# Building weight signs with an OR on VectorE, squaring on VectorE, and a list schedule with other durations, in an attention + two feed-forward layers kernel

## The chip, the cores and the metric

One core of a Trainium2 chip. The metric is the device time of one execution in microseconds (us); the figure to predict is the median of several runs. The engines are called by the profile's names: PE (TensorE), ACT (ScalarE), DVE (VectorE), POOL (GpSimd), SP (the queue that issues the transfers).

## The reference

Attention with 2 x 12 heads, 448 tokens and head size 64, with tanh-capped scores, then two feed-forward layers over 896 tokens. All inputs are fp32.

```python
scores = cap * np.tanh((scale * q @ k.T) / cap)
attn = softmax(scores) @ v            # -> x: 896 tokens x 768
h = x @ w_in                          # 768 x 2048, first layer
x = (np.maximum(h, 0) + alpha * np.minimum(h, 0)) @ w_out
h = x @ w_in2                         # second layer
r = np.maximum(h, 0)
out = (r * r) @ w_out2                # 896 x 768
```

## The kernel before, in words

Attention runs first (to about 102 us of the span), with the first three weight columns of the first layer prepared beside it (`fetch`, `advance`, `up_now`; they use `read`, lines 173 to 185). None of this is touched.

The two layers follow. Work is transposed: features lie on the 128 partitions, tokens (2 halves b of S = 448) in the free dimension. A product of fp32 accuracy is made of three passes of reduced-precision matmuls: weight and token operands are split into a rounded high part (wh, xh, a copy on ACT, line 254) and a rest (wl, xl, a subtraction on DVE, line 257), and `multiply` (line 198) issues high x high, high x low, low x high. The up product of one column group f is 6 x 3 matmuls of 448 tokens for each b, into one PSUM bank (`up`). In the first layer ACT evacuates the bank twice (relu, line 270, and relu of the negative, line 272) and DVE joins them with the slope (line 273). In the second, ACT takes the relu (line 270) and squares it in place (line 276). The down products (`down`) use Strassen-Winograd's seven products of quarter matrices: A11, S3 = A11 - A21, A12 and A22 are loaded as 4 quarters of 4 parts (`quarter`), sums of weights and tokens are DVE additions (line 249), and one product (P1) is done in plain fp32 (line 195) without a split.

The host passes each weight as a 64-bit pattern of which the kernel makes fp32 numbers. A load (`load`, line 219) has five steps: a 768 KB transfer into one of two raw buffers (line 223); ACT multiplies the high words by 2^-112 into w, the rebias (line 239); DVE shifts the low words right by 29 (line 240); ACT writes the sign into the low word, as a 16-bit float with stride four made of the high word times 2^-60 (line 233, called by the operation in line 241); DVE joins, w << 3 | low (line 237). The raw buffer is then free. 61 loads are made this way, 13 + 16 for the up layers and 2 x 16 quarters. There are 16 w buffers, 3 pairs wh/wl outside attention's, 8 PSUM banks and one buffer t.

The order of all this is not written by hand. `layers` describes every operation to `Plan` (`op`), with an engine and a cost in us; `Plan.order` runs a list schedule: an engine that is idle takes, of its operations that are ready and whose buffers are to be had, the one that comes first in the program. A result is ready for others a lag after its end. The instructions are issued in that order, and on the chip each engine keeps it strictly. The costs are `act(n)`, `dve(n)` (two rates) and fixed figures for matmuls (0.2044 us each, 0.752 for a plain fp32 product); the sign is charged like the rebias, act(768) + 0.06 = 0.875 us.

Of the kernel before, what the change touches and what calls it, by code (L numbers as in the profile page):

```python
# [13 lines left out]
ALU = mybir.AluOpType  # L14
# [3 lines left out]
P = 128  # L18
# [10 lines left out]
PARTS = 4  # L29
# [2 lines left out]

PLAIN = ("P1",)

SLOTS = {"raw": 2, "w": 16, "wh": 3, "wl": 3, "g": 35, "t": 1, "xh": 4, "xl": 4}


# [15 lines left out]
class Plan:  # L53
# [4 lines left out]
    def tag(self, name, tiles):  # L58
        self.free[name], self.queue[name] = list(tiles), []

    def op(self, engine, cost, emit, reads=(), writes=(), port=False, lag=0.06):
        op = Op(len(self.ops), engine, cost, emit, port, lag)
        self.ops.append(op)
        before = []
        for buf in reads:
            before.append(buf.writer)
        for buf in writes:
            before += [buf.writer, *buf.readers]
        for other in set(before):
            if other is not None and other is not op:  # L70
                other.feeds.append(op)
                op.needs += 1
        for buf in reads:
            buf.readers.append(op)
        for buf in writes:
            buf.writer, buf.readers = op, []
            if not buf.taken:
                buf.taken = True
                op.takes.append(buf)
                self.queue[buf.tag].append(op)  # L80
        op.bufs = list(dict.fromkeys([*reads, *writes]))
        for buf in op.bufs:
            buf.left += 1

    def order(self):
# [5 lines left out]
        for op in self.ops:  # L91
            if not op.needs:
                heapq.heappush(events, (0.0, op.number, "ready", op))
        while events:
            now = events[0][0]
            while events and events[0][0] <= now:
                _, _, what, op = heapq.heappop(events)
                if what == "ready":
                    heapq.heappush(ready[op.engine], (op.number, op))
                elif what == "end":  # L100
                    for buf in op.bufs:
                        buf.left -= 1
                        if not buf.left and buf.tag:
                            self.free[buf.tag].append(buf.tile)
                    for other in op.feeds:
                        other.needs -= 1
                        if not other.needs:
                            heapq.heappush(events, (now + op.lag, other.number, "ready", other))
# [36 lines left out]
class Net:  # L145
# [65 lines left out]
        self.activate(self.early_g[f], self.early_t, ps, f)  # L211

    def act(self, n):
        return 0.17 + 0.00084 * n

    def dve(self, n, rate=1):
        return 0.16 + 0.00103 * n if rate == 1 else 0.13 + 0.00052 * n

    def load(self, src):

        nc, plan, n = self.nc, self.plan, self.NC * P
        raw, w = Buf("raw"), Buf("w")
        plan.op("SP", 0.06, lambda: nc.sync.dma_start(raw.tile, src), (), [raw], lag=4.0)
        low, high = Buf(), Buf()
        for b in (low, high):
            b.writer = raw.writer

        def parts():
            return self.words(raw.tile)

        def sign():
            halves = raw.tile.bitcast(F16).rearrange("p n (f t) -> p n f t", t=4)
            nc.scalar.mul(halves[:, :, :, 1], parts()[1].bitcast(F32), 2.0 ** -60)  # L233

        def join():
            bits = w.tile.bitcast(I32)
            nc.vector.scalar_tensor_tensor(bits, bits, 3, parts()[0], op0=ALU.logical_shift_left, op1=ALU.bitwise_or)  # L237

        plan.op("ACT", self.act(n) + 0.06, lambda: nc.scalar.mul(w.tile, parts()[1].bitcast(F32), 2.0 ** -112), [high, raw], [w])  # L239
        plan.op("DVE", self.dve(n, 2), lambda: nc.vector.tensor_scalar(parts()[0], parts()[0], 29, None, op0=ALU.logical_shift_right), [raw], [low], port=True)  # L240
        plan.op("ACT", self.act(n) + 0.06, sign, [high, raw], [low])
        plan.op("DVE", self.dve(n), join, [low, w, raw], [w], port=True)
        return w

# [13 lines left out]
        return h, l  # L258

    def products(self, ps, w, x, c, first, last):  # L260
        self.plan.op("PE", 3 * 0.2044 if len(w) == 2 else 0.752, lambda: self.multiply(ps.tile, [b.tile for b in w], [b.tile for b in x], c, first, last),
                     [*w, *x], [ps])

    def up(self, w, f, b, first):

        nc, S, plan, half = self.nc, self.S, self.plan, self.NF // 2
        ps, g, t = Buf("ps"), Buf("g"), Buf("t")
        for c in range(self.NC):
            self.products(ps, w, self.x[b, c], c, c == 0, c == self.NC - 1)
        plan.op("ACT", self.act(S), lambda: nc.scalar.activation(g.tile, ps.tile, AF.Relu), [ps], [g])  # L270
        if first:
            plan.op("ACT", self.act(S), lambda: nc.scalar.activation(t.tile, ps.tile, AF.Relu, scale=-1.0), [ps], [t])  # L272
            plan.op("DVE", self.dve(S), lambda: nc.vector.scalar_tensor_tensor(
                g.tile, t.tile, self.slope_t[:, f:f + 1], g.tile, op0=ALU.mult, op1=ALU.add), [t, g], [g], port=True)
        else:
            plan.op("ACT", self.act(S), lambda: nc.scalar.square(g.tile, g.tile), [g], [g])  # L276
        self.g[b, f] = g
        if b == 1 and f >= half:
            self.sum(self.g[1, f - half], g, self.g[1, f - half], "tensor_sub", S)

    def quarter(self, name, i):
        a = {"A11": 0, "S3": 1, "A12": 2, "A22": 3}[name]
        w = self.a[name, i] = self.load(self.wdown[:, a * PARTS + i])
        if name == "S3":
            self.sum(w, self.a["A11", i], w, "tensor_sub", self.NC * P)

# [73 lines left out]
    def layers(self):  # L360

        both = range(self.B)
        self.x = {(b, j): [Buf(None, t[b][:, j]) for t in (self.xh, self.xl)] for b in both for j in range(self.NC)}
        self.g = {(0, f): Buf(None, self.early_g[f]) for f in range(AHEAD)}
        ahead = []
        for f in range(AHEAD):
            hl = []
            for tag, t in (("wh", self.wh[f]), ("wl", self.wl[f])):
                b = Buf(tag, t)
                b.taken = True  # L370
                hl.append(b)
            ahead.append(hl)
        for first, src, self.wdown in ((True, self.w1, self.w2), (False, self.w3, self.w4)):
            self.a = {}
            for f in range(self.NF):
                early = first and f < AHEAD
                w = ahead[f] if early else self.split(self.load(src[:, f]), ("wh", "wl"), self.NC * P)
                for b in both:
                    if not (early and b == 0):
                        self.up(w, f, b, first)  # L380
            for i in range(PARTS):
                self.quarter("A11", i)
                self.quarter("S3", i)
            for name in ("A12", "A22"):
                for i in range(PARTS):
                    self.quarter(name, i)
            self.down(not first)
        engines = {mybir.EngineType.PE, mybir.EngineType.Activation, mybir.EngineType.DVE, mybir.EngineType.Pool, mybir.EngineType.SP}
        with self.tc.manual_schedule(engines=engines):
            for op in self.plan.order():  # L390
                op.emit()
# [331 lines left out]
    def run(self, fast):  # L723
        self.raws = []
        with ExitStack() as ctx:
            wp = self.pool(ctx, "wp", 1)
            splits = {t: [wp.tile([P, self.NC, P], F32R, name=f"{t}{n}") for n in range(SLOTS[t])] for t in ("wh", "wl")}
            self.wh, self.wl = splits["wh"], splits["wl"]
# [23 lines left out]
            plan.tag("raw", [self.raw[:, (AHEAD + n) % 2] for n in range(2)])  # L752
            plan.tag("w", [lp.tile([P, self.NC, P], F32, name=f"w{n}") for n in range(SLOTS["w"])])
            for t in ("wh", "wl"):
                plan.tag(t, splits[t][AHEAD:])
            plan.tag("t", [self.early_t])
            plan.tag("g", [lp.tile([P, self.S], F32, name=f"g{n}") for n in range(SLOTS["g"])])
            for t in ("xh", "xl"):
                plan.tag(t, [lp.tile([P, self.S], F32R, name=f"{t}{n}") for n in range(SLOTS[t])])
            banks = [hm.tile([P, self.S], F32, name=f"hm{n}", padded_shape=[P, 512]) for n in range(2)]  # L760
# [67 lines left out]
```

## Time and profile before

| | us |
|---|---|
| median of 3 runs | 566.67 |
| lowest to highest | 564.88 to 567.07 |
| the profiled execution | 567.58 |
| its span | 565.8 |
| PE busy | 538.9 (95%) |
| ACT busy | 419.6 (74%) |
| DVE busy | 405.4 (72%) |
| transfers, mean | 114 GB/s |

All durations of the working are from the profiled execution. The 1.8 us between its time and its span lie around the program. A busy PE here means that matmuls are in its pipeline; two records of 370 ns follow each other every 204 ns. The stages are read from the kernel's loops: up products of the first layer from 102 to 219 us, its down products to 323, up products of the second to 449, its down products to 560.

### The profile page before, as it was taken

What the parts mean: (1) busy time and instruction counts of PE and PEld (TensorE: products, weight loads), DVE (VectorE), ACT (ScalarE), POOL (GpSimd) and SP (SyncE); (2) the same over time, 40 slices, a digit from 0 to 9 for tenths busy, and PEclk for the clock granted to TensorE, in tenths of its full rate; (3) what the DMA queues carried; (4) which work ended last, traced back from release to release, by engine and by line L of the source; (5) the groups of instructions that cost most, each with busy time, mean ns of one, the idle gap of its engine ahead of it and who ended that gap; (6) DMA issues with size and microseconds to landing.
All of it is one profiled execution on the core that took longest, in us unless ns stands there. A gap on an engine that the chain in (4) does not pass through costs nothing.

```text
span 565.8 us, 6752 instructions
## 1 busy us (share of the span) xinstructions
PE 538.9 (95%) x2556; PEld 424.9 (75%) x2556; DVE 405.4 (72%) x574; ACT 419.6 (74%) x518; POOL 2.0 (0%) x12
## 2 busy tenths in 40 slices
PE   7889899979999997998999899999999999999996
PEld 2223345969999896758898788999999984789985
DVE  1798999465567767889999964444567579989862
ACT  6999892487889878957655479999889997354550
POOL 1000000000000000000000000000000000000000
PEclk9999999999999999999999899999999999999998
DMA  6455442053454444553000035555444553010111
GB/s 198 175 175 168 133 130 59 0 168 117 162 167 120 160 144 138 166 162 116 1 2 0 0 112 168 167 168 167 137 149 162 167 168 111 2 49 2 49 50 54
DMA packets 19576, 64.23 MB, mean 114 GB/s; under 512 B 3920, under 2 KB 10576, under 8 KB 19536
## 3 DMA queue, kind: packets, MB, share of 16 engines
q1 hardware_dynamic: 19392, 63.72, 34.8%
q8 instruction: 22, 0.36, 0.3%
q14 instruction: 18, 0.15, 0.1%
q10 hardware_dynamic: 144, 0.00, 0.0%
HBM read 60.89 MB, written 2.79 MB: 113 GB/s over the span
## 4 chain that ended last, share of the span: by engine, by line
PE 48%; ACT 28%; DVE 16%; DMA 4%; issue 2%; POOL 0%; ACTq 0%; DVEq 0%; POOLq 0%
PE ps L198 28%; ACT raw L233 14%; PE hm L198 11%; DVE w L237 3%; PE ps L195 3%; ACT wh L254 3%; PE pv L516 3%; ACT w L239 3%; DMA k<-in_kT 2%; DVE wl L257 2%; ACT g L270 2%; PE ps L466 2%; DVE raw L240 2%; DVE w L249 2%; ACT xh L254 1%
## 5 line engine op out<-in xcount | busy, mean ns | idle before, releaser
L198 PE MATMUL ps<-x,wh 128*128 128x448 f32 x576 | 166.6, 370 | 3.9 <-ACT t L272 2.7
L233 ACT ACTIVATE raw<-raw 128x768 f16<-128x768 f32 x61 | 118.5, 1943 | 22.8 <-DVE raw L240 22.8
L237 DVE SCALAR_TENSOR_TENSOR w<-w,raw 128x768 int32<-128x768 int32 x61 | 58.5, 959 | 88.1 <-ACT raw L233 88.0
L198 PEld LDWEIGHTS ps<-x,wh 128*128 128x128 f32 x576 | 108.3, 189 | 17.7 <-ACT t L272 3.6
L198 PE MATMUL ps<-x,wl 128*128 128x448 f32 x288 | 106.4, 369 | 0.4 <-DVE wl L257 0.4
L254 ACT CAST xh<-g 128x448 fp32r<-128x448 f32 x93 | 52.9, 576 | 62.9 <-PE ps L198 40.9
L198 PE MATMUL ps<-xh,wh 128*128 128x448 f32 x224 | 83.9, 374 | 6.7 <-ACT t L272 3.0
L257 DVE TENSOR_TENSOR wl<-w,wh 128x768 fp32r<-128x768 f32 x77 | 73.5, 955 | 16.4 <-ACT wh L254 15.0
L198 PE MATMUL ps<-xl,wh 128*128 128x448 f32 x224 | 82.2, 367 | 0.8 <-DVE xl L257 0.8
L198 PE MATMUL ps<-xh,wl 128*128 128x448 f32 x224 | 82.3, 367 | 0.4 <-DVE wl L257 0.4
L254 ACT CAST wh<-w 128x768 fp32r<-128x768 f32 x77 | 64.8, 842 | 6.4 <-DVE w L237 4.9
L257 DVE TENSOR_TENSOR xl<-g,xh 128x448 fp32r<-128x448 f32 x93 | 56.4, 621 | 11.5 <-ACT xh L254 10.3
L198 PEld LDWEIGHTS ps<-x,wl 128*128 128x128 f32 x288 | 54.5, 189 | 5.3 <-DVE wl L257 0.7
L239 ACT ACTIVATE w<-raw 128x768 f32<-128x768 f32 x61 | 56.1, 919 | 2.0 <-DMA raw<-in_w 2.0
L198 PE MATMUL hm<-x,wh 128*128 128x448 f32 x192 | 54.6, 366 | 0.0
L198 PEld LDWEIGHTS ps<-xh,wh 128*128 128x128 f32 x224 | 42.2, 188 | 14.9 <-ACT t L272 3.6
L198 PEld LDWEIGHTS ps<-xl,wh 128*128 128x128 f32 x224 | 42.2, 189 | 4.7 <-DVE xl L257 1.2
L198 PEld LDWEIGHTS ps<-xh,wl 128*128 128x128 f32 x224 | 42.2, 188 | 4.3 <-DVE wl L257 0.7
L481 ACT ACTIVATE E<-ps,scale_t 128x896 f32<-128x896 f32 x42 | 40.3, 1022 | 5.3 <-PE ps L466 5.3
L249 DVE TENSOR_TENSOR g<-g,g 128x448 f32<-128x448 f32 x64 | 39.0, 620 | 1.0 <-ACT g L276 0.7
L198 PEld LDWEIGHTS hm<-x,wh 128*128 128x128 f32 x192 | 36.0, 187 | 3.4
L486 ACT ACTIVATE E<-E,cap_t 128x1792 f32<-128x1792 f32 (+1 forms) x24 | 38.1, 1617 | 0.0
(96 smaller groups left out, 630.7 us busy)
## 6 DMA issues: line engine op xcount, KB each, us to landing
raw<-in_w SPq DMA_DIRECT2D x64, 768.0 KB, 4.2
out_T<-g SPq DMA_DIRECT2D x12, 224.0 KB, 2.0
k<-in_kT SPq DMA_DIRECT2D x11, 224.0 KB, 4.9
q<-in_qT SPq DMA_DIRECT2D x11, 224.0 KB, 5.1
v<-in_vT SPq DMA_DIRECT2D x6, 384.0 KB, 5.2
rb<-row SPq DMA_DIRECT2D x10, 224.0 KB, 3.7
vt<-in_vt SPq DMA_DIRECT2D x6, 64.0 KB, 5.6
r<-rows SPq DMA_DIRECT2D x20, 1.8 KB, 3.6
```

The lines of the kernel that those rows point to most:

```text
L195: self.nc.tensor.matmul(ps, w[0][:, c, :], x[0], start=first, stop=last)
L198: self.nc.tensor.matmul(ps, a[:, c, :], m, start=first and n == 0, stop=last and n == 2)
L233: nc.scalar.mul(halves[:, :, :, 1], parts()[1].bitcast(F32), 2.0 ** -60)
L237: nc.vector.scalar_tensor_tensor(bits, bits, 3, parts()[0], op0=ALU.logical_shift_left, op1=ALU.bitwise_or)
L239: plan.op("ACT", self.act(n) + 0.06, lambda: nc.scalar.mul(w.tile, parts()[1].bitcast(F32), 2.0 ** -112), [high, raw], [w])
L240: plan.op("DVE", self.dve(n, 2), lambda: nc.vector.tensor_scalar(parts()[0], parts()[0], 29, None, op0=ALU.logical_shift_right), [raw], [l ...
L249: plan.op(engine, cost, lambda: getattr(e, op)(out.tile, a.tile, b.tile), [a, b], [out], port=True)
L254: plan.op("ACT", self.act(n), lambda: nc.scalar.copy(h.tile, w.tile), [w], [h])
L257: lambda: e.tensor_sub(l.tile, w.tile, h.tile.bitcast(F32)), [w, h], [l], port=True)
L481: nc.scalar.activation(es[-1][:, n % 2], ps, AF.Tanh, scale=self.scale_t)
L486: self.nc.scalar.activation(x, x, AF.Exp, scale=self.cap_t)
L516: nc.tensor.matmul(self.pv[u][rows, g, :], self.v[u][0][:, g, c, rows], self.chunk(u, g * FULL + c)[:, e], start=c == 0, stop=False)
```

## The change

- `load` takes a flag, half. Where it is true the load is as before. Where it is false, DVE makes the sign: the high words are ANDed in place with the sign bit (which must come after the rebias has read them), then low = low >> 29 | high in one operation, then the join as before. ACT then has only the rebias.
- `HALF` says which: false for all up loads; for the quarters true for A11 and A12 (a = 0, 2) and false for S3's load and A22 (a = 1, 3).
- `SQ` is false for every f: the square is g = max(ps, 0) * g on DVE, read from PSUM, instead of a square on ACT.
- The planner's figures change: act, dve, the sign's cost (1.68), the matmuls' (0.2038 and 0.746) and the default lag (0.15 for 0.06). Its rules stay.

```diff
+HALF = (lambda f, first: False, lambda i, a: i % 2 == 0)
+SQ = lambda f: False
...
-    def op(self, engine, cost, emit, reads=(), writes=(), port=False, lag=0.06):
+    def op(self, engine, cost, emit, reads=(), writes=(), port=False, lag=0.15):
...
     def act(self, n):
-        return 0.17 + 0.00084 * n
+        return 0.05 + 0.000885 * n
     def dve(self, n, rate=1):
-        return 0.16 + 0.00103 * n if rate == 1 else 0.13 + 0.00052 * n
-    def load(self, src):
+        return 0.075 + 0.00103 * n if rate == 1 else 0.07 + 0.00052 * n
+    def load(self, src, half):
...
-        plan.op("DVE", self.dve(n, 2), lambda: nc.vector.tensor_scalar(parts()[0], parts()[0], 29, None, op0=ALU.logical_shift_right), [raw], [low], port=True)
-        plan.op("ACT", self.act(n) + 0.06, sign, [high, raw], [low])
+        if half:
+            plan.op("DVE", self.dve(n, 2), lambda: nc.vector.tensor_scalar(parts()[0], parts()[0], 29, None, op0=ALU.logical_shift_right), [raw], [low], port=True)
+            plan.op("ACT", 1.68, sign, [high, raw], [low])
+        else:
+            plan.op("DVE", self.dve(n, 2), lambda: nc.vector.tensor_scalar(parts()[1], parts()[1], -(1 << 31), None, op0=ALU.bitwise_and), [raw], [high], port=True)
+            plan.op("DVE", self.dve(n), lambda: nc.vector.scalar_tensor_tensor(
+                parts()[0], parts()[0], 29, parts()[1], op0=ALU.logical_shift_right, op1=ALU.bitwise_or), [raw, high], [low], port=True)
         plan.op("DVE", self.dve(n), join, [low, w, raw], [w], port=True)
...
-        self.plan.op("PE", 3 * 0.2044 if len(w) == 2 else 0.752, ...
+        self.plan.op("PE", 3 * 0.2038 if len(w) == 2 else 0.746, ...
...
-            plan.op("ACT", self.act(S), lambda: nc.scalar.square(g.tile, g.tile), [g], [g])
+            if SQ(f):
+                plan.op("ACT", self.act(S), lambda: nc.scalar.square(g.tile, g.tile), [g], [g])
+            else:
+                plan.op("DVE", self.dve(S) + 0.06, lambda: nc.vector.scalar_tensor_tensor(
+                    g.tile, ps.tile, 0.0, g.tile, op0=ALU.max, op1=ALU.mult), [g, ps], [g])
...
-        w = self.a[name, i] = self.load(self.wdown[:, a * PARTS + i])
+        w = self.a[name, i] = self.load(self.wdown[:, a * PARTS + i], HALF[1](i, a))
...
-                w = ahead[f] if early else self.split(self.load(src[:, f]), ("wh", "wl"), self.NC * P)
+                w = ahead[f] if early else self.split(self.load(src[:, f], HALF[0](f, first)), ("wh", "wl"), self.NC * P)
```

## Rows read from the trace of the kernel before

**Rows 1.** Busy time by stage: length, busy us of PE, PEld, DVE, ACT, POOL, clock, DMA.

```profile
102.00:219.00 117.00, 110.18 (x527) 99.29 (x525) 73.64 (x104) 95.32 (x121) 0.00 (x0) 0.99 0.42 135
219.00:323.00 104.00, 100.32 (x434) 82.02 (x435) 93.23 (x143) 69.47 (x100) 0.00 (x0) 0.99 0.21 69
323.00:449.00 126.00, 125.66 (x612) 114.63 (x612) 69.53 (x96) 111.91 (x137) 0.00 (x0) 1.00 0.47 151
449.00:560.00 111.00, 108.83 (x489) 91.16 (x487) 88.00 (x134) 62.88 (x90) 0.00 (x0) 1.00 0.18 62
```

**Rows 2.** The same table for the two stretches with a low granted clock.

```profile
126.00:130.00 4.00, 4.00 (x15) 3.58 (x14) 2.23 (x4) 2.97 (x4) 0.00 (x0) 0.63 0.16 68
320.00:324.00 4.00, 4.00 (x13) 3.57 (x13) 3.48 (x6) 1.30 (x2) 0.00 (x0) 0.57 0.00 0
```

**Rows 3.** TensorE's timeline, gaps: start, us, instruction, in brackets idle time and releaser.

```profile
114.24 0.68 PE L198 MATMUL ps<-x,wh 128*128 128x448 f32 x2 [0.92 <-ACT wh L254]
...
125.00 0.67 PE L198 MATMUL ps<-x,wh 128*128 128x448 f32 x2 [1.87 <-ACT t L272]
...
186.42 0.68 PE L198 MATMUL ps<-x,wh 128*128 128x448 f32 x2 [0.79 <-ACT t L272]
...
219.10 0.47 PE L198 MATMUL ps<-xh,wh 128*128 128x448 f32 x1 [2.98 <-ACT t L272]
...
256.04 0.47 PE L198 MATMUL ps<-xh,wh 128*128 128x448 f32 x1 [1.44 <-ACT g L332]
...
318.76 0.47 PE L198 MATMUL ps<-xh,wh 128*128 128x448 f32 x1 [1.44 <-ACT wh L254]
```

**Rows 4.** Groups by line and shape: count, busy us, mean ns, idle time before.

```profile
L233 ACT ACTIVATE raw<-raw 128x768 f16<-128x768 f32 x61 | 118.5, 1943 | 22.8 <-DVE raw L240 22.8
...
L239 ACT ACTIVATE w<-raw 128x768 f32<-128x768 f32 x61 | 56.1, 919 | 2.0 <-DMA raw<-in_w 2.0
...
L237 DVE SCALAR_TENSOR_TENSOR w<-w,raw 128x768 int32<-128x768 int32 x61 | 58.5, 959 | 88.1 <-ACT raw L233 88.0
...
L240 DVE TENSOR_SCALAR raw<-raw 128x768 int32<-128x768 int32 x61 | 33.9, 556 | 0.1
...
L276 ACT ACTIVATE g<-g 128x448 f32<-128x448 f32 x32 | 18.6, 581 | 0.4
...
L181 DVE TENSOR_SCALAR raw<-raw 128x768 int32<-128x768 int32 x3 | 1.6, 530 | 0.0
...
L183 DVE SCALAR_TENSOR_TENSOR raw<-raw 128x768 int32<-128x768 int32 x3 | 3.0, 992 | 0.1
```

**Rows 5.** ScalarE's timeline near 110 and near 217.

```profile
109.07 0.54 ACT L270 ACTIVATE g<-hm 128x448 f32<-128x448 f32 x1 [4.89 <-PE hm L198]
...
110.36 1.95 ACT L233 ACTIVATE raw<-raw 128x768 f16<-128x768 f32 x1
112.03 0.65 ACT L272 ACTIVATE t<-hm 128x448 f32<-128x448 f32 x1
...
216.35 1.90 ACT L233 ACTIVATE raw<-raw 128x768 f16<-128x768 f32 x1 [0.90 <-DVE raw L240]
218.00 0.62 ACT L270 ACTIVATE g<-ps 128x448 f32<-128x448 f32 x1
```

**Rows 6.** Waits of the SP queue: total us, times, longest.

```profile
SPq L223 <- DVE w L237: 353.3, 59, 66.0
```

**Rows 7.** VectorE's timeline: additions from SBUF, and the last ones from PSUM.

```profile
293.43 1.15 DVE L249 TENSOR_TENSOR g<-g,g 128x448 f32<-128x448 f32 x2
...
559.05 1.86 DVE L329 TENSOR_TENSOR g<-ps,g 128x448 f32<-128x448 f32 x3 [4.97 <-PE ps L198]
```

**Rows 8.** Line 239 (rebias, one per load) by stage: busy us (count).

```profile
102.00:219.00 117.00, 19.38 (x21) 0.99 0.42 135
219.00:323.00 104.00, 9.27 (x10) 0.99 0.21 69
323.00:449.00 126.00, 21.46 (x24) 1.00 0.47 151
449.00:560.00 111.00, 5.97 (x7) 1.00 0.18 62
```

More of the change, by code (lines that the diff above doesn't have):

```diff
@@ L260, in products @@
     def products(self, ps, w, x, c, first, last):
-        self.plan.op("PE", 3 * 0.2044 if len(w) == 2 else 0.752, lambda: self.multiply(ps.tile, [b.tile for b in w], [b.tile for b in x], c, first, last),
+        self.plan.op("PE", 3 * 0.2038 if len(w) == 2 else 0.746, lambda: self.multiply(ps.tile, [b.tile for b in w], [b.tile for b in x], c, first, last),
                      [*w, *x], [ps])
```

## The prediction

> **What bounds the kernel now.** I first read the table by stage, because the share over the span mixes stages. The layers run from 102 to 560 us in four stages: up products of the first layer (102 to 219), its down products (219 to 323), and the same for the second layer (323 to 449, 449 to 560). In all four TensorE (PE) is busy 94% to 99.7% of the stage [rows 1], so it sets the end, and the only thing an edit on other engines can return is PE's lost time. That has two parts. Idle time is stage length less busy time: 117 - 110.18 = 6.8 us, 104 - 100.32 = 3.7, 126 - 125.66 = 0.3, 111 - 108.83 = 2.2, together 13.0. The other part is work at a low clock: two stretches of 4 us behind idle gaps were granted 0.63 and 0.57 of full speed [rows 2], that is between the levels of 2.4 and 1.2 GHz, and cost 4 x 0.37 = 1.5 and 4 x 0.43 = 1.7 us. So 13.0 + 3.2 = 16.2 us is the ceiling of any gain here. What lies before 102 us (attention) is not touched, nor the end: VectorE's (DVE's) last three adds begin at 559.05 [rows 7], and with PE done by 560, adds and output transfers fill the 5.8 us that are left of the span.
>
> Next I looked for the gaps one by one in PE's timeline [rows 3]. The reader is to see the releaser in brackets: nearly all name ScalarE (ACT), either an evacuation of a PSUM bank (t L272, g L332) or a split of weights (wh L254). The six largest are 0.79 to 2.98 us, 9.4 of the 13.0 us of idle time.
>
> Why is ACT late? Per load of weights it does a rebias (L239), a sign (L233) and, for what is split, a copy (L254); the sign takes 1943 ns where the rebias, reading the same words, takes 919 [rows 4]. But the planner that wrote the order charged the sign like the rebias: 0.17 + 0.00084 x 768 + 0.06 = 0.875 us. So the order was made for an ACT that is about 1 us per sign faster than the real one, 61 times. An engine works strictly in order; what stands behind a sign is late. Seen at 218: the evacuation L270 starts where the sign of 216.35 lets go [rows 5], and PE, which waits for the evacuations behind it, stands still for 2.98 us.
>
> **The signs.** 13 + 16 up loads and 16 of the 32 quarter loads change, 45 of 61. ACT loses 45 x 1.943 = 87.4 us. DVE loses the shift L240 (556 ns) and gets an AND and an OR; the attention part already runs both on the same tiles, at 530 and 992 ns (L181, L183) [rows 4]. So DVE gains 0.530 + 0.992 - 0.556 = 0.966 us a load, 43.5 us in all.
> The chain of one load changes too. Before, rebias and shift go side by side, then sign and join: 0.919 + 1.943 + 0.959 = 3.82 us. After, the AND overwrites the words that the rebias reads, so it waits for it, which is new: 0.919 + 0.530 + 0.992 + 0.959 = 3.40, without the semaphore steps. Behind the waiting AND stand the join and the splits of other loads on DVE. The chain is 0.4 us shorter if DVE is free, and has one step on ACT instead of two. SP issues the next transfer only when the join has let go of one of two raw buffers: its queue waited for the join 353.3 us in 59 waits [rows 6]. So a shorter hold brings the transfers forward; the bound is from 0.4 us sooner to some tenths later per load, if DVE is the one that makes it wait. No extra transfer is issued.
>
> **The squares.** 32 squares leave ACT (581 ns, 18.6 us). DVE does max(ps, 0) x g in one operation, which nothing in the trace does; bounds are the SBUF product L249 (two in 1.15 us: 0.53 from start to start) and the add that reads PSUM (three in 1.86: 0.62 each) [rows 7]. I take 0.62, as it reads PSUM: 32 x 0.62 = 19.8 us. The bank is held until then, no longer only until the relu.
>
> **Where this falls.** Rebiases per stage are 21, 10, 24, 7 (one straddles 449) [rows 8]. Of the 10 in the second stage two already belong to the next layer, so eight quarters come there (A12 and A22, of which four change); of the 21, 13 up loads and four of eight quarters change. In the third stage 16 up loads and four quarters change, in the fourth four.
> - 102 to 219: ACT 95.3 - 17 x 1.943 = 62 us of 117; DVE 73.6 + 17 x 0.966 = 90.
> - 219 to 323: ACT 69.5 - 7.8 = 62 of 104; DVE 93.2 + 3.9 = 97, unless the quarters arrive before 219.
> - 323 to 449: ACT 111.9 - 20 x 1.943 - 30 x 0.58 = 56 of 126; DVE 69.5 + 20 x 0.966 + 30 x 0.62 = 107.
> - 449 to 560: ACT 62.9 - 9 = 54 of 111; DVE 88.0 + 3.9 + 1.2 = 93.
> No stage is over its length on either engine, and ACT, which PE waited for, becomes the light one. In the second stage DVE is the one to watch.
>
> A rule of the Trainium skill speaks against this part: ScalarE: Activation LUTs, section What ACT_TABLE_LOAD costs, has an ACTIVATE pass one element per cycle for fp32 and bf16 alike, 186 ns + 0.833 ns each. By it a sign would cost 0.83 us (an estimate from that page), ACT would be relieved of 37 us only, the load chain would grow, and the result would be that of the second rival. The trace disagrees for this 16-bit strided write: 1943 ns over 61 records [rows 4].
>
> **New durations.** The planner now charges 1.68 for the sign, and less per operation with a longer lag: a split 0.073 x 10 = 0.73 + 0.15, against 0.815 + 0.06. From 110.36 to the next start at 112.03 the sign really holds ACT 1.67 us [rows 5]. This part has no price of its own; it moves where stalls fall.
>
> **The sum, gap by gap** [rows 3]. 114: the first sign starts only at 110.36, behind evacuations that waited until 109.07 [rows 5]; with AND and OR on DVE the chain no longer queues there: 0.7 of 0.9 us back. 125: the third weights; 1.87 idle and 1.5 clock, 3.0 back. 186: 0.8. 219: 2.5 of 3.0. 256 (evacuation behind a sign): 1.4. 318: DVE forms the weight sum too late, then 1.44 idle and 1.7 clock; quarters that land sooner empty DVE ahead of it, half back: 1.6. Fourth stage: 1.0 of 2.2. Together 11.0. Against it, new waits on DVE; nothing shows them, I take two of 0.7, like the smallest large gap: 1.4. What is late next is DVE's weight sums and splits. Net 9.6 us. Profiled execution: 567.58 - 9.6 = 558.0. The median of the three timed runs lies 0.9 below that execution, so 557.1.
>
> **Rivals.**
> 1. The load chain doesn't get shorter, because AND, OR and join queue on DVE. Only evacuation gaps return (0.8 + 2.5 + 1.4 + 1.0 = 5.7) less 1.4: 4.3 back, 562.4. For it: DVE is 90% busy from 219 on [rows 1]. Against: 63% in the first stage, where the loads matter.
> 2. What the up stage returns is lost in the down stages: DVE has 104 - 93.2 = 10.8 us of slack there and gets 3.9 more. Then 318's wait with its clock (3.1) stays, and one more of its size comes in each layer: 11.0 - 1.6 - 6.2 - 1.4 = 1.8 back, 564.9. Against: the fourth stage carries the same DVE work at 79%.
> 3. Slower: squares and ORs in the third stage. PE loses nothing there now. DVE's queue goes to 107 of 126 us; squares release the banks in order behind ANDs that wait for a rebias. If PE waits 0.8 us (the gap at 186) at each of 16 weight groups, 12.8 us, and the clock falls twice (3.4), that is 16.2 lost against 11.0 - 1.4 = 9.6 returned, 6.6 us slower: 573.3. It decides from the point where DVE's work and waits exceed 126 us, 18 more than reckoned. Against: eight banks, two in use at a time.
>
> **How the numbers follow.** Forecast 0.60, rivals 0.18, 0.12, 0.10. A measurement of this kernel can tell about 0.5%, 2.8 us, from no change; faster means under 563.8. Forecast and rival 1 are faster: 0.78; rival 2 same: 0.12; rival 3 slower: 0.10. The range begins at 551, nearly the whole ceiling (566.7 - 16.2 = 550.5), and ends at 566, which takes in the first two rivals and leaves the third out.
>
> **What would show it.** Right: L233 16 times, PE's idle time from 102 to 219 under 3 us, no stretch at half clock near 126, ACT about 56 us in the third stage, DVE about 107, more than 21 rebiases before 219. Wrong: PE waiting for DVE (squares, AND) in the third stage, more than two new waits over 0.7 us, the gap near 318 as long as before or longer, or AND, OR or square well over 0.53, 0.99 and 0.68 us.

## The result, and the profile after

The changed kernel takes 551.6 us (median of four runs), the kernel before 565.77 in the same sessions: ratio 0.975, 95% interval 0.9705 to 0.9795. That is 14.2 us less, where 9.6 were forecast; the time lies at the lower end of the range. In a later session the same kernel gave 551.48 us, ratio 0.9733 (0.9706 to 0.976).

The profiled execution took 550.29 us with a span of 548.4. First the page's busy times (us, share of the span, instructions):

```profile
PE 532.6 (97%) x2556; PEld 422.4 (77%) x2556; DVE 460.9 (84%) x651; ACT 327.1 (60%) x441; POOL 2.0 (0%) x12
```

Next the table by stage, with bounds moved so that each stretch holds nearly the same matmuls as in [rows 1] (530, 438, 611 and 485 against 527, 434, 612 and 489); columns as there:

```profile
100.00:209.00 109.00, 108.46 (x530) 98.61 (x529) 87.94 (x119) 65.25 (x104) 0.00 (x0) 1.00 0.44 139
209.00:310.00 101.00, 98.75 (x438) 81.27 (x437) 97.76 (x151) 63.70 (x96) 0.00 (x0) 1.00 0.24 77
310.00:435.00 125.00, 124.76 (x611) 114.16 (x610) 101.79 (x144) 62.13 (x85) 0.00 (x0) 1.00 0.47 152
435.00:543.00 108.00, 107.60 (x485) 90.57 (x483) 92.90 (x141) 55.97 (x84) 0.00 (x0) 1.00 0.19 64
```

The stages are 8, 3, 1 and 3 us shorter. PE's idle time is 0.5 + 2.3 + 0.2 + 0.4 = 3.4 us where it was 13.0 [rows 1], and the clock is full in all four: the two slow stretches [rows 2] are gone. DVE is now 97% busy in the second stage, and PE still loses only 2.3 us there. The gaps that are left, from PE's timeline (start, us, instruction, idle time and releaser), beside [rows 3]:

```profile
178.59 0.68 PE L202 MATMUL ps<-x,wh 128*128 128x448 f32 x2 [0.54 <-ACT t L281]
...
260.76 0.47 PE L202 MATMUL ps<-xl,wh 128*128 128x448 f32 x1 [1.04 <-DVE xl L266]
...
302.87 0.47 PE L202 MATMUL ps<-xh,wh 128*128 128x448 f32 x1 [0.79 <-ACT x L333]
```

The gaps at 114, 125, 219 and 256 have no counterpart. That at 178 is what is left of the gap at 186; the one at 302 waits for the split of a token tile (x), so it is another wait than that for weights (wh) at 318. What the new and the rewritten operations cost, from the groups by line and shape:

```profile
L249 DVE SCALAR_TENSOR_TENSOR raw<-raw 128x768 int32<-128x768 int32 x45 | 43.0, 955 | 0.9
...
L237 ACT ACTIVATE raw<-raw 128x768 f16<-128x768 f32 x16 | 31.2, 1949 | 4.1 <-DVE raw L245 4.1
...
L248 DVE TENSOR_SCALAR raw<-raw 128x768 int32<-128x768 int32 x45 | 25.0, 555 | 1.5 <-ACT w L243 1.5
...
L288 DVE SCALAR_TENSOR_TENSOR g<-ps,g 128x448 f32<-128x448 f32 x24 | 14.9, 621 | 7.7 <-ACT g L279 7.7
```

AND and OR take 555 and 955 ns, together 1.51 us where 1.522 were reckoned. The square from PSUM lasts 0.62 us in the record; how long it holds DVE is another figure, to which the point on costs comes back. The line of the squares has 24 of the 32; the other eight, from banks called hm, last 620 ns.

One part of the difference between the two profiled executions is not the change's. The first planned product of the layers begins 2.3 us earlier in the second one, though attention is the same program. The two lines, the first of the kernel before, the second of the changed one:

```profile
102.12 0.57 PE L198 MATMUL hm<-x,wh 128*128 128x448 f32 x2
```

```profile
99.84 0.57 PE L202 MATMUL hm<-x,wh 128*128 128x448 f32 x2
```

In the traces of the twelve other runs, with the same attention, it begins at 99.83 to 101.29, so the trace of the kernel before is the late one. So of the 17.4 us between the spans, 15 are the layers': 9.6 of idle time, 3.2 of low clock, and some 2 that these rows don't place. The medians, over several runs each, differ by 14.2.

### The profile page after: what moved, and what is told of

It is laid out like the page before. It is cut to its first block, busy times and chain, and to the rows that moved or that the text cites. A ratio compares the mean times of both kernels' runs of the same rounds, so it can differ in the third digit from the quotient of the medians.

```text
span 548.4 us, 6811 instructions
## 1 busy us (share of the span) xinstructions
PE 532.6 (97%) x2556; PEld 422.4 (77%) x2556; DVE 460.9 (84%) x651; ACT 327.1 (60%) x441; POOL 2.0 (0%) x12
## 4 chain that ended last, share of the span: by engine, by line
PE 79%; DVE 11%; ACT 5%; issue 2%; DMA 1%; POOL 0%; DVEq 0%; ACTq 0%; POOLq 0%
PE ps L202 49%; PE hm L202 14%; PE ps L199 4%; PE pv L529 4%; PE ps L479 3%; DVE xl L266 3%; PE hm L199 2%; DVE wl L266 2%; ACT E L494 1%; ACT E L499 1%; DMA k<-in_kT 1%; DVE g L342 1%; DVE ps L342 1%; DVE w L258 1%; ACT raw L237 1%
## 5 line engine op out<-in xcount | busy, mean ns | idle before, releaser
L263 ACT CAST wh<-w 128x768 fp32r<-128x768 f32 x77 | 64.3, 837 | 40.4 <-PE ps L202 16.2
L279 ACT ACTIVATE g<-ps 128x448 f32<-128x448 f32 x45 | 24.6, 547 | 41.6 <-PE ps L202 41.4
L249 DVE SCALAR_TENSOR_TENSOR raw<-raw 128x768 int32<-128x768 int32 x45 | 43.0, 955 | 0.9
```

Of the source, the lines that this page charges most:

```text
L249: plan.op("DVE", self.dve(n), lambda: nc.vector.scalar_tensor_tensor(parts()[0], parts()[0], 29, parts()[1], op0=ALU.logical_shift_right, ...
L263: plan.op("ACT", self.act(n), lambda: nc.scalar.copy(h.tile, w.tile), [w], [h])
```

## The experiments

The change has two halves: what moves to DVE (signs, squares), and the planner's figures, which move nothing but make another order. The prediction gave the moves 11.0 us and the figures no price of their own. Theory A, the prediction's: PE waited because ACT had too much work. Theory B: it waited because the order was made with a sign charged 0.875 us that takes 1.94.

**The figures alone.** All signs and squares stay on ACT:

```diff
-HALF = (lambda f, first: False, lambda i, a: i % 2 == 0)
-SQ = lambda f: False
+HALF = (lambda f, first: True, lambda i, a: True)
+SQ = lambda f: True
```

> The changed planner figures alone: every sign and every square stays on ScalarE. Theory A (TensorE waited because ScalarE had too much work standing in front of evacuations and splits): ScalarE keeps its 340 us of work in the layers, so the time stays at 560 to 566 us, against 565.8 before. Theory B (the order was wrong because a sign was charged 0.875 us and took 1.94): the right durations alone give most of the gain, 556 us or less.

Measured: 552.34 us, ratio 0.9788 (0.9759 to 0.9818). Theory A falls. By stage, first two:

```profile
100.00:217.00 117.00, 116.54 (x570) 106.10 (x569) 78.81 (x112) 98.54 (x127) 0.00 (x0) 1.00 0.42 136
217.00:317.00 100.00, 97.49 (x433) 80.43 (x432) 93.32 (x146) 73.39 (x100) 0.00 (x0) 1.00 0.27 87
```

In the first stretch ACT (fourth busy time) works 98.5 of 117 us, more than before [rows 1] (the stretch now holds 570 matmuls and not 527), and PE stands idle 0.5 us. So an ACT as full as before did no harm here; what differs is the order of its work. One such place in ACT's timeline:

```profile
101.15 0.90 ACT L243 ACTIVATE w<-raw 128x768 f32<-128x768 f32 x1
102.49 1.95 ACT L237 ACTIVATE raw<-raw 128x768 f16<-128x768 f32 x1 [0.44 <-DVE raw L245]
106.99 0.54 ACT L279 ACTIVATE g<-hm 128x448 f32<-128x448 f32 x1 [2.56 <-PE hm L202]
```

The first sign now stands ahead of the evacuation that waits for PE. In the order before it stood behind it, and began at 110.36 after 4.89 us of waiting [rows 5].

**The moves alone.** The change with the old figures, the 16 signs left on ACT charged 0.875 again:

```diff
-    def op(..., lag=0.15):
-        return 0.05 + 0.000885 * n
-        return 0.075 + 0.00103 * n if rate == 1 else 0.07 + 0.00052 * n
-            plan.op("ACT", 1.68, sign, [high, raw], [low])
-        ... 3 * 0.2038 if len(w) == 2 else 0.746
+    def op(..., lag=0.06):
+        return 0.17 + 0.00084 * n
+        return 0.16 + 0.00103 * n if rate == 1 else 0.13 + 0.00052 * n
+            plan.op("ACT", self.act(n) + 0.06, sign, [high, raw], [low])
+        ... 3 * 0.2044 if len(w) == 2 else 0.752
```

> Signs and squares on VectorE as in the change, but the planner keeps its old figures, the 16 signs left on ScalarE at 0.875 us again. Theory A: most of the gain is there, 551 to 556 us. Theory B: the gain is lost, 561 us or more.

Measured: 564.66 us, ratio 0.9994 (0.9972 to 1.0016): no gain, as theory B expected. In the first stage PE loses only 0.9 us now, as was reckoned from ACT's relief, but it loses 5.7 us in the second and 3.6 in the third, where it lost 3.7 and 0.3 before [rows 1]. The first three stretches of the table:

```profile
100.00:217.00 117.00, 116.07 (x567) 105.51 (x566) 93.13 (x128) 70.43 (x111) 0.00 (x0) 1.00 0.42 135
217.00:317.00 100.00, 94.30 (x402) 75.61 (x401) 90.71 (x140) 59.33 (x88) 0.00 (x0) 0.98 0.22 71
317.00:443.00 126.00, 122.45 (x590) 109.64 (x589) 97.96 (x138) 59.77 (x83) 0.00 (x0) 1.00 0.42 138
```

The largest gap of the second stretch, on PE, and the start of the second layer on DVE and PE:

```profile
263.31 0.47 PE L202 MATMUL ps<-xh,wh 128*128 128x448 f32 x1 [2.50 <-ACT wh L263]
...
323.78 0.63 DVE L342 TENSOR_TENSOR ps<-ps,g 128x448 f32<-128x448 f32 x1 [0.19 <-PE ps L202]
324.39 1.24 DVE L342 TENSOR_TENSOR hm<-hm,g 128x448 f32<-128x448 f32 x2
325.54 0.61 DVE L334 TENSOR_TENSOR x<-ps,x 128x448 fp32r<-128x448 f32 x1
326.07 1.14 DVE L334 TENSOR_TENSOR x<-hm,x 128x448 fp32r<-128x448 f32 x2
327.13 0.95 DVE L266 TENSOR_TENSOR wl<-w,wh 128x768 fp32r<-128x768 f32 x1
...
328.13 0.47 PE L202 MATMUL ps<-x,wl 128*128 128x448 f32 x1 [2.77 <-DVE wl L266]
```

The weights' low part comes last on DVE, behind three additions (L342) and three token splits (L334) of the layer's end, and PE waits 2.77 us for it. With 98 of 126 us DVE isn't full there; the order is what is late.

**Squares and signs apart, with the new figures.** Squares back on ACT (`SQ = lambda f: True`):

> The change with its durations, but the squares stay on ScalarE. In the third stage TensorE lost only 0.3 us before and ScalarE has some 73 us of work in 126 without the signs, so theories A and B both expect the time of the changed kernel, 551.6 within 1.5 us. If the squares mattered (rival: the relief of ScalarE in the third stage), 555 us or more.

Measured: 553.87 us, ratio 0.9799 (0.9768 to 0.9831), 0.8 us over the upper bound of theories A and B and below the rival's 555. And squares on DVE with all signs on ACT (`HALF` true throughout):

> New durations and the squares on VectorE, all signs on ScalarE. Theory A: the first layer, where most of the lost time lies, keeps its full ScalarE, so as the kernel with durations alone within 2 us, 559 to 566 us. Theory B: 556 us or less, as with durations alone.

Measured: 552.73 us, ratio 0.9782 (0.9756 to 0.9808), as theory B expected. The intervals of both overlap with that of the figures alone. With the new figures it hardly matters which of the two engines does this work.

**Which figure?** The kernel before with the sign's charge alone set to 1.68:

> The kernel before with one figure changed: the sign on ScalarE is charged 1.68 us and not 0.875. Theory C (the gain of the durations is that of the sign's charge, 61 signs that came 0.8 us late each): 555 us or less. Theory D (it is that of the other figures, the rates and the lag): 561 us or more. In between, both have a share.

Measured: 559.74 us, ratio 0.9893 (0.9863 to 0.9922), half of the gain, between the two theories. The kernel before with everything but that:

> The kernel before with all the new figures (rates, lag, matmuls) except the sign, which stays charged like the rebias (0.73 + 0.06 = 0.79 us). Theory C: no gain, 561 us or more, perhaps slower than before as the sign is then charged even less. Theory D: 555 us or less.

Measured: 567.28 us, ratio 1.0024 (1.0004 to 1.0044), none of it, as theory C expected. So the rates and the lag are worth nothing without the sign's charge and some 6 us beyond it (0.9893 to 0.9788). To see from the other side whether the old order is bad in itself, the sign was left out of the code and left in the plan:

```diff
-        plan.op("ACT", self.act(n) + 0.06, sign, [high, raw], [low])
+        plan.op("ACT", self.act(n) + 0.06, lambda: None, [high, raw], [low])
```

> The kernel before in its own order, with no sign written at all (the signs of the 61 loaded weights are left out); the planner still charges 0.875 us for each, so order and buffers are those of before and ScalarE has 118 us less to do. If the real length of the signs against their charge is what hurts the old order (theory C, and the first prediction's reading that ScalarE is late), 555 us or less. If the old order is bad for other reasons (theory D), 560 us or more.

Measured: 551.49 us, ratio 0.9731 (0.9702 to 0.9759). Its first stretch, and the one gap over 0.5 us that is left:

```profile
100.00:217.00 117.00, 116.81 (x570) 106.04 (x569) 82.51 (x118) 64.31 (x109) 0.00 (x0) 1.00 0.46 147
```

```profile
306.64 0.47 PE L198 MATMUL ps<-xh,wh 128*128 128x448 f32 x1 [1.44 <-ACT wh L254]
```

In the very order of before PE loses 0.2 us here once the signs are gone. This run takes away the whole sign, though, and not only what it lasts beyond its charge, so by itself it fits theory A as well (ACT has less to do). With the figures alone, where ACT has all its work and the gain comes too (552.34), the reading is that the signs hurt where the plan doesn't reckon with them. A run with signs that last just their 0.875 us isn't there.

The gap that is left is that of 318 in the order before [rows 3], as long as there. So it doesn't come from the signs. In the kernel before, the two operations on ACT ahead of it are

```profile
317.41 0.57 ACT L254 CAST xh<-g 128x448 fp32r<-128x448 f32 x1 [1.25 <-PE hm L198]
317.88 0.83 ACT L254 CAST wh<-w 128x768 fp32r<-128x768 f32 x1
```

The weights that PE waits for were summed on DVE by 316.94, but their split stands behind a token split that waits for PE.

The changed kernel, run beside these:

> The changed kernel itself once more, to set it beside the kernel with the durations alone (552.34 us): if signs and squares on VectorE are worth anything on top of the durations, it is 550.5 us or less; if not, 551 to 553 us.

Measured: 551.48 us, ratio 0.9733 (0.9706 to 0.976), beside 0.9788 (0.9759 to 0.9818) of the figures alone. The time lies where it was expected if the moves add nothing (551 to 553). The ratios differ by 0.0055, some 3 us, and the intervals touch at their ends, so these runs don't settle whether signs and squares on DVE add anything.

**How exact must the figures be?** The changed kernel with only the sign's charge undone, 16 signs at 0.79 instead of 1.68:

> The changed kernel with one figure undone: the 16 signs that stay on ScalarE are charged like the rebias, 0.73 + 0.06 = 0.79 us, not 1.68. Theory C (the sign's charge makes the order): with 16 undercharged signs in place of 61, a quarter of the 13 us that the charge is worth with the other new figures, so 553 to 556 us. Theory E (ScalarE now has so much room that an undercharged sign harms nobody): 550.5 to 552.5 us.

Measured: 559.89 us, ratio 0.9882 (0.9852 to 0.9912), worse than both expectations, though ACT has 40% of its time free. The largest gap, on DVE and on PE:

```profile
255.97 0.96 DVE L249 SCALAR_TENSOR_TENSOR raw<-raw 128x768 int32<-128x768 int32 x1
256.84 0.62 DVE L266 TENSOR_TENSOR xl<-g,xh 128x448 fp32r<-128x448 f32 x1
257.37 0.95 DVE L241 SCALAR_TENSOR_TENSOR w<-w,raw 128x768 int32<-128x768 int32 x1
258.24 0.96 DVE L266 TENSOR_TENSOR wl<-w,wh 128x768 fp32r<-128x768 f32 x1
259.11 1.69 DVE L342 TENSOR_TENSOR ps<-ps,g 128x448 f32<-128x448 f32 x3
...
259.88 0.71 PE L202 MATMUL ps<-xh,wh 128*128 128x448 f32 x1 [3.12 <-DVE ps L342]
```

PE's last matmul before the gap starts at 256.40, and the additions that it needs stand behind an OR, a join and two splits. In the changed kernel the same three additions waited only for PE:

```profile
256.17 1.77 DVE L342 TENSOR_TENSOR ps<-ps,g 128x448 f32<-128x448 f32 x3 [0.40 <-PE ps L202]
```

Of DVE's lateness the trace shows one wait for an undercharged sign close ahead of the gap:

```profile
249.01 0.96 DVE L241 SCALAR_TENSOR_TENSOR w<-w,raw 128x768 int32<-128x768 int32 x1 [0.68 <-ACT raw L237]
```

From there DVE works without a pause until the additions. That the rest comes from the other order which the wrong charge made is argued, not shown.

The changed kernel with the old rates and lag, the sign charged 1.68:

> The changed kernel with the old rates, lag and matmul figures, but the sign charged 1.68; beside the kernel with the moves only (564.66 us) it differs in the sign's charge alone. Theory C: the charge is what was missing, 556 us or less. Theory F (with VectorE as the fuller engine its own charge, 0.95 us for 0.87 held, and the short lag spoil the order): 561 us or more.

Measured: 571.41 us, ratio 1.0099 (1.0064 to 1.0133): slower than with the sign undercharged (0.9994), against theory C. The time is what theory F expected; that DVE's charge and the short lag are the reason isn't shown. Its gaps are of the kinds above (2.77 us for weights' low parts at 331.61, 1.93 at 264.26 for a token split). Last, the sign's charge with one of the other two figures, on the kernel before. With the rates:

> The kernel before with the sign charged 1.68 and the new rates of both engines, but the old lag of 0.06. The sign alone gave 559.7, all figures 552.3. If the rates are the other half: 552 to 555 us. If the lag is: 558 us or more. A rate without its lag makes a chain look shorter than it is (0.87 + 0.06 against 0.96 + 0.06 measured), so it may also be worse than the sign alone.

Measured: 555.69 us, ratio 0.9811 (0.9778 to 0.9844). With the lag:

> The kernel before with the sign charged 1.68 and the new lag of 0.15, but the old rates. If the lag is the other half of the gain: 552 to 555 us. If the rates are, or only both together: 558 us or more.

Measured: 557.72 us, ratio 0.9844 (0.9813 to 0.9876). Neither lies in a range that was expected. Each ratio lies between that of the sign alone (0.9893) and that of all figures (0.9788), so both seem to have a share of the other half; how large each is can't be told.

Taken together, with the old kernel as 1:

| | signs and squares on ACT | on DVE, as in the change |
|---|---|---|
| old figures | 1 | 0.9994 |
| old figures, sign at 1.68 | 0.9893 | 1.0099 |
| new figures, sign as the rebias | 1.0024 | 0.9882 |
| new figures | 0.9788 | 0.975, 0.9733 |

A rival to all of this is chance: each set of figures gives one order, and an order may be lucky. Against it, the four orders made with all new figures, wherever signs and squares stand, lie at 0.973 to 0.980, and the eight with an old figure or the sign charged as the rebias, the kernel before included and the run without signs left aside, at 0.981 to 1.010.

## Why the prediction was right or wrong, point by point

- **What bounds the kernel: right.** PE's lost time was all there was to get. 16.2 us were named as the ceiling; 12.8 of them came back (9.6 of 13.0 idle, all 3.2 of the low clock). Some 2 us more of the layers' 15 are in neither part.
- **Why ACT is late: half right.** The prediction saw that the sign was charged 0.875 and took 1.943, and that evacuations stood behind it. The run with the charge corrected confirms it: that alone returns half of the gain of all figures. The excess is 0.8 us a sign and not "about 1", as 1.67 is what it holds ACT. The reading doesn't cover the gap at 318, which stays when the signs are left out; nor does "DVE forms the weight sum too late", as the sum was ready and its split stood behind a token split. And the prediction went on as if the cure were less work on ACT.
- **The sum: the direction and the ceiling hold, the terms don't.** The 11.0 us of gaps were credited to the signs and squares. These alone, in an order made with the old figures, are worth nothing (0.9994): the first stage gives back 5.9 us of idle time, and the second and third lose 5.2 more. The step that failed is the part on the new durations, "This part has no price of its own; it moves where stalls fall": alone it is worth 13 us, and without it the rest is worth nothing. To have measured from the trace that charge and length differ, and by how much, and then not to price the correction, was the error. That 551.6 us still lies in the range, near its lower end, is luck as far as the terms go: the range reached down to the ceiling, and what gave the time back was the term without a price.
- **Gaps given back only in part: too cautious.** In the trace after, five of the six gaps are gone and 0.54 is left of that at 186. Two new waits have come, 1.04 (DVE xl) and 0.79 (ACT x), 1.8 us where 1.4 were taken for them. They are not the price of the moves: with the figures alone a wait of 1.04 for DVE's xl stands at 260.44 too. The rows account for 12.8 us returned against 9.6 forecast. Three slips changed nothing: the fourth stage has gaps of 0.82 (459.26) and 0.87 us (467.50), so 0.79 isn't among the six largest, and DVE is 90% busy in the second stage only, not "from 219 on" (55% in the third, 79% in the fourth [rows 1]), and a split's charge of 0.73 is 0.05 + 0.000885 x 768.
- **Costs of the operations: right but for the square.** 1.51 us for AND and OR against 1.522. DVE in the third stage 101.8 us, forecast 107. ACT 62, forecast 56. The square was priced at 0.62 held, from three adds in 1.86 us [rows 7]. Those three waited for PE's banks one after the other (the last matmul ends at 560.26 us, the third add starts at 560.29); where the banks were ready, adds from PSUM follow each other every 0.53 us, as from SBUF, and the square too lets the next operation start after 0.54. The first line is of the kernel before, the other two of the changed one:

```profile
529.42 2.22 DVE L329 TENSOR_TENSOR g<-ps,g 128x448 f32<-128x448 f32 x4
```

```profile
328.45 0.61 DVE L288 SCALAR_TENSOR_TENSOR g<-ps,g 128x448 f32<-128x448 f32 x1
328.99 0.55 DVE L248 TENSOR_SCALAR raw<-raw 128x768 int32<-128x768 int32 x1
```

  Lengths that overlap by 0.09 us were added up as if they followed each other, which is part of the 5 us that the forecast of DVE's time is too high.
- **Rival 1: its premise doesn't hold in the first layer.** There the 13 up loads, from the start of the rebias to the end of the join in the timelines, take 4.0 us (median) against 4.5 before, about the 0.4 less that was reckoned. The transfers came forward little all the same: 21 rebiases in the first stage as before, where more were expected, and SP waited 343.8 us for the join in 59 waits, before 353.3 [rows 6], the lines of the changed kernel being

```profile
100.00:209.00 109.00, 19.05 (x21) 1.00 0.44 139
```

```profile
SPq L227 <- DVE w L241: 343.8, 59, 55.5
```

  The gaps credited to faster loads (125, 318) went. With the figures alone they went too, with the signs on ACT; so they were gaps of order, which the first sign and the split behind the token split show.
- **Rivals 2 and 3.** DVE did become the fullest engine of the second stage (97%), and 1.04 us was lost there to a wait for it. With wrong figures the same work on DVE gives 559.89 to 571.41 us. The moves with the old figures (564.66) are what rival 2 describes, down to its time (564.9): what the first stage returns is lost behind it. So the losses of both rivals exist, but they come with the order and not with the load of the engine.
- **The rule on ACTIVATE** (Trainium skill, ScalarE: Activation LUTs, What ACT_TABLE_LOAD costs): the 16 remaining signs again take 1949 ns, so the trace goes on disagreeing with one element per cycle for this write.

What stays open: how the gain beyond the sign's charge is shared between rates and lag; why the changed kernel with old rates and lag is slower with the right charge for the sign than with the wrong one; and whether the moves add anything to the figures. A list schedule can change its order everywhere when one figure changes, so single orders can differ by 1% (0.9994 against 1.0099 for the sign's charge) without a term that accounts for it.

## What to carry to other kernels

Where an order comes from a planner, compare each of its charges with the trace first: how long the operation holds its engine (start to start) and when its result is ready (end to the next engine's start). Here one operation was charged 0.875 us and held its engine 1.67 (1.94 in the record), 61 times. The shift of work alone returned nothing; correcting this charge together with the others returned 13 us without moving any work, and correcting it by itself half of that. Price such a correction as a change of its own, by the gaps that stand behind the mischarged operation; and change all figures together, since half-corrected sets gave between 0.981 and 1.010.

## What the runs showed of the hardware that was not expected

DVE kept up at 97% of the second stage with PE losing 2.3 us of 101, so an engine off the bound may be nearly full if its order is right. An OR with two 32-bit inputs of 768 elements with stride two took 955 ns, as long as a plain subtraction of 768 (952). So no cost of that stride shows on DVE, where a 16-bit write with stride four takes ACT 1.95 us against 0.91 for the rebias; whether that is the stride or the type isn't separated. The lines of the subtraction and the rebias, in the changed kernel:

```profile
L266 DVE TENSOR_TENSOR wl<-w,wh 128x768 fp32r<-128x768 f32 x77 | 73.2, 952 | 12.6 <-ACT wh L263 11.6
...
L243 ACT ACTIVATE w<-raw 128x768 f32<-128x768 f32 x61 | 55.7, 914 | 13.1 <-DMA raw<-in_w 12.1 <-DVE wl L266 0.7
```

In the run with the cheap sign the 3.12 us gap was followed by four microseconds at half clock (granted 0.50, that is 1.2 GHz):

```profile
259.00:263.00 4.00, 3.12 (x8) 2.81 (x9) 2.42 (x5) 1.03 (x3) 0.00 (x0) 0.50 0.63 197
```

while the gap of 2.98 us before 219 in the kernel before [rows 3] was followed by none:

```profile
219.00:223.00 4.00, 3.90 (x18) 3.40 (x19) 3.96 (x7) 3.58 (x7) 0.00 (x0) 1.00 0.59 197
```

And the gap of 1.44 us at 318 was followed by a granted 0.57 in the kernel before [rows 2]; behind the same gap of the same order, at 306.64 in the run without signs, the clock stayed at 2.4 GHz:

```profile
308.00:312.00 4.00, 4.00 (x21) 3.72 (x20) 4.00 (x7) 1.87 (x3) 0.00 (x0) 1.00 0.02 4
```

The length of a gap alone did not tell whether the clock fell.
